# A windowed attention and an S4 convolution on one core: the planner's ranked stages replaced by one written instruction sequence per engine, with the first chunk's powers made in place, u·D kept in SBUF and QKV made by block of positions

## The chip, the cores and the metric

The kernel runs on one core of one Trainium2 chip. The metric is device time in microseconds of that core. The engines are TensorE (PE, with its weight loads shown apart as PEld), VectorE (DVE), ScalarE (ACT), GpSimd (POOL) and SyncE (SP, which here only issues DMAs).

## The reference, cut to what matters

Two independent parts, written side by side into one output of 2048 x 1280 (bf16).

```python
# A: 32 heads of 20, each position looks at 8 earlier ones, 2 apart
qkv = (x @ wqkv)                       # x 2048x640, wqkv 640x1920
idx = pos[:, None] - 2 * arange(8)
logits = einsum("bhsd,bhswd->bhsw", q, k[idx]) * 20 ** -0.5   # masked where idx < 0
a = einsum("bhsw,bhswd->bhsd", softmax(logits), v[idx]) @ wo

# B: per channel a kernel of length 2048 from 192 complex modes, then a causal convolution
P = exp(dt * A[:, :, None] * l)        # 640 channels x 192 modes x 2048
K = einsum("dn,dnl,dn->dl", C, P, dt * B).real
b = irfft(rfft(u padded) * rfft(K padded))[:2048] + u * Dskip
```

## The kernel before

Part B goes in five chunks c of 128 channels. **prep** turns the parameters into a log-magnitude `ta` and a phase `wi` (transposed by matmuls, `flip`). **am** and **gens** make the powers of exp(dt·A) for eleven exponents 2^k: ACT does an Exp and two Sin per exponent, DVE three instructions, and the result goes to the DRAM tensor `Gd`. They run twice, for chunks 0 and 1 and for chunks 2 to 4. Per chunk, **tab** and **taby** fetch the powers from `Gd` into the tables `Xg` and `Y`. **xtab** (32 DVE instructions) builds `X`, **ypos** and **yneg** (DVE) and **mag** (ACT) build the rest of `Y`. `X` has two buffers, `Xg` and `Y` have one. **kgen** multiplies X and Y in four quarters, each one zeroing matmul and 128 small ones (33 columns), and each matmul comes with its own weight load. Then POOL shuffles the result `Kd`. **u**, **spread**, **spec** (a two-step transform by matmuls, evicted by ACT), **swap** (DMA), **prod** (four DVE multiplies) and **inv** follow for each chunk. **last0** (chunks 0 to 2, spectra `Z` read back from DRAM into one buffer) and **last1** (chunks 3 and 4) make the outputs; each quarter reads its piece `uq` of u again and DVE multiplies it by Dskip.

Part A: **k0..v4** compute Q, K and V, one column block of 128 over all 2048 positions at a time, and store them in DRAM. For each of four blocks b of 512 positions, **fetch** and **fetchv** read q, k and v back (10 and 20 DMAs), **logits** has ten DVE multiplies (2048 columns) with 40 matmuls, a softmax on ACT and a DVE scaling, **av** has ten more DVE multiplies with 160 matmuls, and **out** projects by `wo`. The multiplies write one of three buffers (tag `pr`), which the matmuls then read. The pool `att` takes the memory of the prep pool, the pool `fft` that of the QKV pool, and the pool `inv` that of the tables.

Which instruction comes next on an engine is settled before the launch: a planner walks all instructions and takes ready ones by the rank of their stage in `ORDER`. Each engine then runs its list in order and waits on semaphores. Exp and Sin on ACT are pinned in program order because they use different tables.

## Time and profile before

| | |
|---|---|
| time, median of 3 runs | 466.06 us (463.52 to 466.42) |
| time recorded for the profiled execution, and its core's span | 465.34 us, 463.6 us |
| span on the page and in the trace | 468.0 us |
| mean granted TensorE clock in the trace | 0.828 of 2.4 GHz |
| busy: PE, DVE, ACT, POOL | 341.5, 309.3, 260.9, 36.7 us |

All stretches and rows are in microseconds from the start of the 468.0 us span. The profiled execution's recorded time is 2.7 us below that span, and the median of the runs is 0.7 us above the recorded time.

### The profile page before, as it was taken

To read this page: it belongs to the slowest core of one execution; us is meant where nothing else is said; L and a number is where in the kernel's file an instruction comes from. 1 tells how busy PE (TensorE), PEld (TensorE's weight loads), DVE (VectorE), ACT (ScalarE), POOL (GpSimd) and SP (SyncE) were. 2 spreads that over 40 slices of the span, in tenths; PEclk is the share of its full clock that TensorE was granted. 3 is DMA by queue.
4 is the path that set the end of the run, shared out by engine and by line. 5 is a ranking of instruction groups with operands and counts; after the bars stand their busy time and mean duration, and the time that the engine had idled before them with its cause. 6 is when DMAs were issued, how large, how long until landed. Compare 5 with 4: busy or idle time off the path is not lost.

```text
span 468.0 us, 13264 instructions
## 1 busy us (share of the span) xinstructions
PE 341.5 (73%) x5672; PEld 214.7 (46%) x5684; DVE 309.3 (66%) x448; ACT 260.9 (56%) x570; POOL 36.7 (8%) x80
## 2 busy tenths in 40 slices
...
GB/s 236 210 210 192 289 243 272 104 154 171 272 255 255 152 241 112 29 19 77 243 53 124 71 23 178 55 120 85 106 207 166 368 94 121 74 1 158 219 157 110
DMA packets 90378, 72.86 MB, mean 156 GB/s; under 512 B 44528, under 2 KB 82656, under 8 KB 88656
## 3 DMA queue, kind: packets, MB, share of 16 engines
...
## 4 chain that ended last, share of the span: by engine, by line
PE 38%; DVE 20%; DMA 16%; issue 12%; ACT 8%; SPq 4%; ACTq 0%; DVEq 0%; POOL 0%; POOLq 0%
PE ps_p L471 10%; PE ps_k L355 6%; PE ps_k L350 6%; PE ps_ia L435 4%; DVE prod L524 4%; DVE p L554 4%; DMA Gdram<-cs 4%; DMA zq<-Zdram 3%; PE ps_ib L803 3%; SPq L453 3%; DMA kd<-st 2%; DVE krtmp L265 2%; ACT mag L307 2%; ACT Sp L412 2%; DMA Xg<-Gdram 2%
## 5 line engine op out<-in xcount | busy, mean ns | idle before, releaser
L471 PE MATMUL ps_p<-xT,w 128*128 128x512 bf16 x288 | 80.2, 421 | 24.3 <-ACT st L472 15.8
L471 PEld LDWEIGHTS <-w 128*128 128x128 bf16 x300 | 30.1, 105 | 63.0 <-issue 33.9
L524 DVE TENSOR_TENSOR prod<-qb,kb 128x2048 bf16<-128x2048 bf16 x40 | 47.3, 1217 | 7.1 <-PE ps_l L528 6.0
L472 ACT CAST st<-ps_p 128x512 bf16<-128x512 f32 x60 | 34.2, 585 | 31.7 <-PE ps_p L471 23.3
L554 DVE TENSOR_TENSOR p<-vb,attn 128x2048 bf16<-128x2048 bf16 x40 | 47.1, 1217 | 2.1 <-PE ps_o L560 2.0
L408 PE MATMUL ps_f<-A,cT 64*128 64x128 bf16 (+1 forms) x768 | 36.4, 230 | 16.3 <-ACT Sp L412 8.6
L394 ACT CAST A<-ps_f 128x512 bf16<-128x512 f32 x80 | 42.1, 614 | 8.3 <-PE ps_f L393 8.1
L412 ACT CAST Sp<-ps_f 128x512 bf16<-128x512 f32 (+1 forms) x96 | 42.8, 579 | 6.0 <-PE ps_f L408 5.9
L355 PE MATMUL ps_k<-Ytab,Xtab 64*20 64x33 bf16 x1280 | 28.3, 244 | 20.2 <-issue 20.2
L408 PEld LDWEIGHTS <-cT 64*128 64x128 bf16 x768 | 31.0, 105 | 25.5 <-issue 24.7
L357 ACT CAST Kd<-ps_k 128x264 bf16<-128x264 f32 x20 | 7.5, 379 | 61.7 <-PE ps_k L355 61.7
L796 DVE TENSOR_TENSOR uq<-uq,Dsb 128x1536 bf16<-128x1536 bf16 (+1 forms) x8 | 6.6, 825 | 50.7 <-DMA uq<-Udram 37.4
L560 PE MATMUL ps_o<-p,cHs 64*32 64x256 bf16 x640 | 31.2, 308 | 11.4 <-DVE p L554 10.1
L436 ACT CAST Z<-ps_ia 128x512 bf16<-128x512 f32 x40 | 21.6, 594 | 29.6 <-PE ps_ia L435 29.5
L355 PEld LDWEIGHTS <-Xtab 64*20 64x20 bf16 x1280 | 22.3, 124 | 26.3 <-issue 24.3
L350 PE MATMUL ps_k<-Ytab,Xtab 128*20 128x33 bf16 x1280 | 28.1, 249 | 5.4 <-issue 5.4
L435 PE MATMUL ps_ia<-cE,Sp 128*128 128x128 bf16 x160 | 23.7, 244 | 9.7 <-DVE Sp L423 9.7
L350 PEld LDWEIGHTS <-Xtab 128*20 128x20 bf16 x1280 | 22.6, 128 | 12.8 <-issue 11.2
L573 PE MATMUL ps_op<-wo,oT 128*128 128x320 bf16 x160 | 27.9, 321 | 0.0
L307 ACT ACTIVATE mag<-ta 128x192 bf16<-128x192 f32 x80 | 21.7, 353 | 10.4 <-DVE Ytab L313 10.4
L264 DVE TENSOR_TENSOR Ytab<-Ytab 128x384 bf16<-128x384 bf16 (+2 forms) x15 | 13.3, 888 | 21.4 <-DMA Ytab<-Gdram 21.1
L528 PE MATMUL ps_l<-prod,cGs 128*32 128x512 bf16 x160 | 24.7, 420 | 3.2 <-DVE prod L524 3.0
...
## 6 DMA issues: line engine op xcount, KB each, us to landing
...
```

Of the source, the lines that this page charges most:

```text
L307: pin(self.nc.scalar.activation(out=self.mg[b // 8][:, b % 8], in_=ta[:, s], func=ACT.Exp, scale=-16.0 * (b + 1)))
L350: MM(o, lhsT=X[:, :, part, col], rhs=Y[:, :, part, col], start=False, stop=False, tile_position=(0, 32 * g), skip_group_check=True)
L355: MM(o, lhsT=X[hb:hb + 64, :, part - 2, col], rhs=Y[hb:hb + 64, :, part - 2, col], start=False, stop=(part == 3), tile_position=(hb, 32 * ...
L394: nc.scalar.copy(out=A1[:].rearrange("p k r s t -> p (k r) s t")[:, :, sig, 8 * q:8 * q + 8], in_=ps[:])
L408: nc.tensor.matmul(ps[h][:, kk], lhsT=C["T"][hs, k, 64 * (1 - r):64 * (1 - r) + 128], rhs=A1[hs, k, r, s0:s1, :].rearrange("p s t -> p (s ...
L412: nc.scalar.copy(out=o, in_=ps[h][:].rearrange("p k (s t) -> p s t k", t=64))
L435: nc.tensor.matmul(ps[:, i], lhsT=X[:, h, 4 * t:4 * t + 4, :].rearrange("p g k -> p (g k)"), rhs=C["E"][:, n_, :], start=(i == 0 and n_ == ...
L471: nc.tensor.matmul(ps[:], lhsT=self.w[which][:, kt, 128 * ct:128 * ct + 128], rhs=self.xT[:, kt, 512 * sc:512 * sc + 512], start=(kt == 0) ...
L472: nc.scalar.copy(out=st[:, sc], in_=ps[:])
L524: V.tensor_tensor(out=pr[:], in0=q[ct][:].unsqueeze(1).to_broadcast([128, 4, PB]), in1=windows(k[ct][:, 8 - 8 * wg:8 - 8 * wg + PB], 2, 4) ...
L554: V.tensor_tensor(out=p2[:], in0=windows(self.v[b][t][:, 2 * qp:2 * qp + 2, 0:PH], 2, 4), in1=at[:].unsqueeze(2).to_broadcast([128, 4, 2, ...
L560: nc.tensor.matmul(ps[half][32 * q:32 * q + 32, t % 2], lhsT=C["Hs"][r], rhs=p2[r, m, q2, :], start=(t % 2 == 0 and m == 0), stop=(m == 3) ...
```

## The change

`ORDER` goes. `SEQ` lists for PE, ACT, DVE, POOL and SP the stages in the order in which their instructions run, with counts: "xtab3:10" is the next ten instructions of that stage on that engine. `chain` ties each engine's instructions together in that order without semaphores.

- gens runs for chunk 0 alone and for chunks 1 to 4 together. Chunk 0's powers are written straight into `Y` and `Xg` (`here`), the others through `Gd` as before (`away`).
- Q, K and V are made by block of 512 positions (`proj(nm, sc)`), five column blocks at a time. q and k share one DRAM tensor. A block's fetch takes 5 DMAs where it took 10, its fetch of v 8 where it took 20; the two tiles of v have one buffer each.
- The loads and stores of u and the loads of HB go from SP's queue to POOL's, the loads of wqkv from POOL's to ACT's.
- u is read once into `uD` (20 KB per partition) and multiplied by Dskip in five DVE instructions of 2048 columns, in place of eight reads and eight multiplies. last0 goes in eight pieces with two halves of a buffer for the spectra.
- `flip` uses one matmul of 128 columns in place of two of 64. kgen's four quarters are stages of their own (kgen20 to kgen23 for chunk 2).

```diff
-ORDER = """
-k4 am2 inv4 v0 weights k0 u1 spec2 am0 q3 tab2 tab4 v3 prep load taby2 ypos1 ypos0 out1 xtab2 xtab0 tab1 tab0 q2 q1 swap1 k1 yneg1 load2 v2
...
+SEQ = {
+    mybir.EngineType.PE: """
...
+spec:15 out0:3 logits1:2 u1:8 logits1:2 out0:2 u1:2 out0:2 u1:2 out0 u1:2 logits1:4 u1:2 out0:2 spread0:8 out0:2 spread0:8 logits1:2 spread0:20
...
+out0:3 spec0:16 out0:2 spec0:15 out0 spec0:48 inv0:57 kgen20:129 inv0:7 logits1:8 kgen21 kgen22 kgen23:33 u2:2 logits1:2 kgen23:32 u2:2 logits1:2
+kgen23:64 u2:2 kgen22:32 u2:2 kgen22:32 u2:4 kgen22:64 u2:4 kgen21:128 spread1:36 av1:6 spread1:8 av1:5 spread1:2 av1:8 spread1:2 av1:9 spread1:2
+av1:9 spread1:2 av1:27 spec1:49 av1:15 spec1:16 av1 spec1:63 inv1:64 kgen30 kgen31:33 kgen30:32 kgen31:96 kgen30:96 kgen32 kgen33 u3:2 kgen33:32 u3:2
+kgen33:32 u3:2 kgen33:32 u3:4 kgen33:32 kgen32:32 u3:6 kgen32:32 spread2:16 kgen32:32 spread2:20 kgen32:32 av1:21 spread2:8 av1:5 spread2:2 av1:8
+spread2:4 av1:2 spread2:2 av1:12 spec2:6 logits2:4 spec2:26 av1:8 spec2 av1:19 spec2:16 av1:5 logits2:4 spec2:31 out1:2 logits2:4 spec2 out1:2
+spec2:16 out1 spec2:15 out1:2 spec2 out1:3 spec2:15 out1:20 inv2:32 out1:7 inv2:25 kgen40:33 inv2:5 logits2:4 inv2:2 out1:2 kgen40:96 logits2:4 out1
...
+out2:2 spec4:15 logits3:4 spec4 out2:2 spec4:15 logits3:4 out2:20 inv4:32 out2 logits3:4 out2:5 inv4:25 last00:18 inv4:7 logits3:12 out2:5 last01
+logits3:2 last01:8 logits3:2 last01 last02 last01:8 last02:17 last03 av3:32 last03:9 last04 last03:8 av3:17 last04:17 av3:37 last05 av3:39 last05:17
+av3:35 last06:10 out3:10 last06:8 out3:10 last07 out3:10 last07:17 last10:34 last11:17 out3:10 last11:17 last12:34 last13:34
+""",
...
+    mybir.EngineType.DVE: """
...
+xtab1:4 logits0 xtab1:4 logits0 xtab1:2 logits0 ypos1:2 logits0 ypos1:2 logits0 ypos1:2 logits0 ypos1:4 yneg1 ypos1:2 yneg1:2 u xtab2:2 yneg1 xtab2:2
+logits0 xtab2:2 logits0 xtab2:2 logits0 xtab2:2 logits0 xtab2:8 logits0 xtab2 av0:8 xtab2 av0:2 xtab2 ypos2 xtab2 logits1 xtab2:4 logits1 xtab2:4
+logits1 xtab2:2 logits1 ypos2 logits1 ypos2:2 logits1 ypos2:2 logits1 ypos2:2 logits1 ypos2 xtab3 ypos2 yneg2 ypos2:2 yneg2 xtab3 yneg2 prod0 xtab3
+prod0:2 xtab3 prod0 xtab3:2 yneg2 xtab3:2 logits1 xtab3:2 logits1 xtab3:10 logits1 xtab3:2 av1 xtab3:4 av1 xtab3:4 av1 xtab3:2 ypos3:4 av1 ypos3:2
+xtab4 ypos3:2 av1 ypos3:2 yneg3 ypos3:2 yneg3 xtab4 prod1 xtab4 prod1:2 xtab4 prod1 xtab4:2 yneg3 xtab4:2 yneg3 xtab4:2 av1 xtab4:2 av1 xtab4:2 av1
+xtab4:18 av1:2 ypos4:2 logits2 ypos4:4 logits2 ypos4:2 logits2 yneg4 ypos4 yneg4 ypos4 prod2 ypos4 prod2:2 ypos4 prod2 yneg4 logits2 yneg4 logits2:7
+av2:7 prod3:3 av2 prod3 av2 ud1 ud4 ud0 ud2 ud3 av2 logits3:6 prod4:3 logits3 prod4 logits3:4 av3:10
+""",
+    mybir.EngineType.Pool: """
+load ypos0 load:6 prep:18 load:7 ypos0 u:13 load2:4 u ypos1:2 kgen03:4 u:6 logits0:7 ypos2:2 kgen13:4 ypos3:2 kgen23:4 ypos4:2 kgen33:4 hb kgen43:4
+hb:3
+""",
+    mybir.EngineType.SP: """
+prep:12 load:15 weights k0 weights genm1:2 q0 genm1 v0 genm1:2 k1 genm1:3 q1 genm1:2 v1 genm1 k2 tab1 fetchv0:8 fetch0:2 q2 fetch0 taby1:5 v2 tab2
...
+    mybir.EngineType.SP: """
...
+inv0 swap1 u3 taby3:3 tab4 taby3:2 fetchv2:4 swap2:2 inv1 u4 taby4:5 fetchv2:4 fetch2 out1:3 fetch2 swap3:2 inv2 fetch3 out1 fetch3:2 last00:3
+last01:3 fetchv3:4 ud swap4:2 fetchv3:4 fetch3:2 out2:3 last02:3 last00:4 out2 last03:3 last04:3 last01 last02:4 last01 last05:3 last06:3 last01:2
+last03:4 last07:3 last04:4 last05:4 out3:2 last06:4 last07:2 out3 last07:2 out3 last10:4 last11:4 last12:4 last13:4
+""",
+}
+
...
-        ph = gp.tile([128, 3 * CW], i32, name="ph", tag="ph", bufs=2)[:, 0:n * CW]
-        ab = gp.tile([128, 3 * CW], f32, name="ab", tag="ab", bufs=2)[:, 0:n * CW]
-        cs = gp.tile([128, 3, 2, CW], bf16, name="cs", tag="cs", bufs=4)[:, 0:n]
+        ph = gp.tile([128, 4 * CW], i32, name="ph", tag="tmp4", bufs=4)[:, 0:n * CW]
+        ab = gp.tile([128, 4 * CW], f32, name="ab", tag="tmp4", bufs=4)[:, 0:n * CW]
+        cs, done = put(k)
         V.tensor_scalar(out=ph, in0=wi[:, s], scalar1=k + 1, scalar2=None, op0=A.logical_shift_left)
         v = lambda ap: ap.rearrange("p (c n) -> p c n", c=n)
...
-        V.tensor_tensor(out=cs, in0=cs, in1=v(am[:, k]).unsqueeze(2).to_broadcast([128, n, 2, CW]), op=A.mult)
-        (nc.sync if ca else nc.scalar).dma_start(out=Gd[ca:cb, :, G_SLOTS.index(2 ** k)].rearrange("c p r n -> p c (r n)"), in_=cs.rearrange("p c r n -> p c (r n)"))
+        with scaled():
+            V.tensor_tensor(out=cs, in0=cs, in1=v(am[:, k]).unsqueeze(2).to_broadcast([128, n, 2, CW]), op=A.mult)
+            if done:
+                done(cs)
...
+    def proj(self, which, sc):
...
+        for ct in range(5):
...
+            nc.scalar.copy(out=st[:, ct], in_=ps[:])
+        s = slice(HALO + 512 * sc, HALO + 512 * sc + 512)
+        if which == "v":
+            nc.sync.dma_start(out=self.vd[:].rearrange("h d i -> (h d) i").rearrange("(c p) i -> p c i", p=128)[:, :, s], in_=st[:])
...
+            t = p.tile([128, 2, HALO + PB], bf16, name="qk", tag="qk", bufs=3)
+            nc.sync.dma_start(out=t[:], in_=self.qkd[:, ct, :, i0:i0 + PB + HALO])
+            self.qk[b].append(t)
...
+        for i, (d0, n) in enumerate(((0, 8), (8, 12))):
+            v = p.tile([128, n, PH + 6], bf16, name="vb", tag=f"vb{i}", bufs=1)
...
+
+        for engine, text in SEQ.items():
+            left = {name: iter(made) for (e, name), made in ((k, v) for k, v in placed.items() if k) if e == engine}
+            last = None
+            for word in text.split():
+                name, _, n = word.partition(":")
+                for _ in range(int(n or 1)):
+                    ins = next(left[name])
+                    if last is not None:
+                        tc.add_manual_dep(ins, last.name, mybir.DependencyInfo(mybir.DependencyClass.NoSync, mybir.DependencyReason.DATA), reason="order of the stages")
+                    last = ins
...
+    def here(k):
+        t = tabs[0]
+        return (t.Y[:, 16 + 2 ** (k - 3)] if 3 <= k <= 7 else t.Xg[:, k if k < 3 else k - 5]).unsqueeze(1), None
+
+    def away(k):
+        cs = pp.tile([128, 4, 2, CW], bf16, name="cs", tag="cs", bufs=4)
+        return cs[:], lambda cs: nc.sync.dma_start(out=Gd[1:NCH, :, G_SLOTS.index(2 ** k)].rearrange("c p r n -> p c (r n)"), in_=cs.rearrange("p c r n -> p c (r n)"))
...
-                nc.sync.dma_start(out=us[32 * g:32 * g + 32], in_=usrc[g, :, s])
+                nc.gpsimd.dma_start(out=us[32 * g:32 * g + 32], in_=usrc[g, :, s])
...
+    with at("ud"):
+        nc.sync.dma_start(out=uD[:].rearrange("p x l t -> p (x l t)"), in_=Ud[:].rearrange("p x l t -> p (x l t)"))
+    for x in range(0, 2 * NCH, 2):
+        with at(f"ud{x // 2}"):
+            dv = Dsb[:, 16 * x:16 * x + 32].rearrange("p (x t) -> p x t", t=16).unsqueeze(2).to_broadcast([128, 2, 64, 16])
...
+    zb = fp.tile([128, 128, 32], bf16, name="zb", tag="Z")[:].rearrange("p x t -> p (x t)")[:, 0:2 * 1536].rearrange("p (b c x t) -> p b c x t", b=2, c=3, t=32)
+    for e in range(8):
+        with at(f"last0{e}"):
+            for i in range(3):
+                nc.sync.dma_start(out=zb[:, e % 2, i], in_=Zd[i][:, 16 * e:16 * e + 16])
+            inverse([0, 1, 2], zb[:, e % 2], 8 * e, 8)
```

## Rows read from the trace of the kernel before

**Rows 1.** The page's first part: busy time, share of the span and instructions of each engine.
```profile
PE 341.5 (73%) x5672; PEld 214.7 (46%) x5684; DVE 309.3 (66%) x448; ACT 260.9 (56%) x570; POOL 36.7 (8%) x80
```

**Rows 2.** Stages: engine busy us (instructions), granted clock (2.4 GHz = 1), DMA share, GB/s.
```profile
0.00:17.00 17.00, 3.46 (x34) 2.20 (x34) 1.31 (x7) 5.75 (x12) 10.57 (x25) 1.00 0.89 237
17.00:156.00 139.00, 109.27 (x1344) 53.88 (x1355) 116.41 (x212) 86.91 (x182) 15.58 (x27) 0.85 0.81 215
156.00:222.00 66.00, 43.86 (x748) 29.90 (x742) 56.12 (x79) 39.58 (x93) 3.18 (x13) 0.74 0.42 105
222.00:243.00 21.00, 13.68 (x465) 9.77 (x453) 1.44 (x5) 4.20 (x9) 2.63 (x6) 0.67 0.56 160
...
289.00:305.00 16.00, 11.18 (x342) 7.50 (x334) 0.39 (x3) 3.71 (x8) 2.62 (x6) 0.62 0.38 114
...
341.00:368.00 27.00, 17.53 (x578) 12.98 (x577) 2.75 (x3) 8.70 (x21) 2.17 (x4) 0.68 0.75 230
368.00:420.00 52.00, 45.01 (x776) 31.04 (x776) 41.63 (x37) 38.02 (x86) 0.00 (x0) 0.93 0.38 111
420.00:468.00 48.00, 29.97 (x400) 22.62 (x400) 8.43 (x10) 18.38 (x40) 0.00 (x0) 0.81 0.70 157
```

**Rows 3.** Timeline, DVE: start, length, instruction, then idle before it and its releaser.
```profile
214.16 1.22 DVE L423 TENSOR_TENSOR Sp<-Sp 128x2048 bf16<-128x2048 bf16 x1
...
242.49 0.36 DVE L264 TENSOR_TENSOR Ytab<-Ytab 128x384 bf16<-128x384 bf16 x1 [3.22 <-DMA Ytab<-Gdram]
...
278.42 1.22 DVE L423 TENSOR_TENSOR Sp<-Sp 128x2048 bf16<-128x2048 bf16 x1
...
304.69 0.36 DVE L264 TENSOR_TENSOR Ytab<-Ytab 128x384 bf16<-128x384 bf16 x1 [15.61 <-DMA Ytab<-Gdram]
...
337.27 1.21 DVE L423 TENSOR_TENSOR Sp<-Sp 128x2048 bf16<-128x2048 bf16 x1
```

**Rows 4.** Timeline, PE, first three quarters of kgen for chunk 2.
```profile
220.05 0.29 PE L343 MATMUL ps_k<-Ytab,zw 128*128 128x264 bf16 x1
...
228.29 0.65 PE L355 MATMUL ps_k<-Ytab,Xtab 64*20 64x33 bf16 x25 [3.33 <-issue]
...
234.48 0.65 PE L355 MATMUL ps_k<-Ytab,Xtab 64*20 64x33 bf16 x26 [3.23 <-issue]
```

**Rows 5.** Timeline, PE, end of kgen for chunk 4.
```profile
360.00 0.45 PE L355 MATMUL ps_k<-Ytab,Xtab 64*20 64x33 bf16 x16 [3.28 <-issue]
```

**Rows 6.** Groups by line, DVE: count | busy us, mean ns | idle before.
```profile
L524 DVE TENSOR_TENSOR prod<-qb,kb 128x2048 bf16<-128x2048 bf16 x40 | 47.3, 1217 | 7.1 <-PE ps_l L528 6.0 <-PE ps_o L560 1.1
...
L264 DVE TENSOR_TENSOR Xtab<-Xtab,Xg 128x768 bf16<-128x768 bf16 (+2 forms) x35 | 24.5, 699 | 0.5
...
L268 DVE TENSOR_TENSOR Xtab<-Xtab,krtmp 128x384 bf16<-128x384 bf16 (+2 forms) x40 | 16.2, 406 | 0.5
...
L796 DVE TENSOR_TENSOR uq<-uq,Dsb 128x1536 bf16<-128x1536 bf16 (+1 forms) x8 | 6.6, 825 | 50.7 <-DMA uq<-Udram 37.4 <-PE ps_ib L800 7.6 <-PE ps_ib L803 5.7
```

**Rows 7.** Waits of the whole span: total us, times, longest us.
```profile
ACT cs L248 <- DMA Gdram<-cs: 8.3, 5, 4.4
...
DVE cs L251 <- ACT cs L250: 5.9, 4, 3.4
```

**Rows 8.** Timeline, DVE, two single waits.
```profile
178.47 0.36 DVE L264 TENSOR_TENSOR Xtab<-Xg 128x384 bf16<-128x384 bf16 x1 [6.04 <-DMA Xg<-Gdram]
...
406.38 1.23 DVE L542 TENSOR_TENSOR attn<-attn,rc 128x1024 bf16<-128x1024 bf16 x1 [7.64 <-ACT rc L541]
```

**Rows 9.** Timeline, PE, the last 32 us.
```profile
436.83 1.52 PE L573 MATMUL ps_op<-wo,oT 128*128 128x320 bf16 x10
...
447.60 2.72 PE L803 MATMUL ps_ib<-zq,HB 128*128 128x96 bf16 x32 [5.20 <-DMA zq<-Zdram]
...
453.92 0.63 PE L803 MATMUL ps_ib<-Z,HB 128*128 128x64 bf16 x16
...
461.82 1.06 PE L803 MATMUL ps_ib<-Z,HB 128*128 128x64 bf16 x16
```

More of the change, by code (lines that the diff above doesn't have):

```diff
@@ L135, in att_consts_np @@
     return dict(Gs=gs.reshape(128, 160), Hs=hs, Sm=sm)
-ORDER = """
-k4 am2 inv4 v0 weights k0 u1 spec2 am0 q3 tab2 tab4 v3 prep load taby2 ypos1 ypos0 out1 xtab2 xtab0 tab1 tab0 q2 q1 swap1 k1 yneg1 load2 v2
-mag2 u0 yneg0 fetch0 v4 q0 spread0 k2 tab3 mag0 kgen2 mag1 gens0 kgen4 last13 q4 fetch1 spec1 inv0 kgen1 kgen0 u2 ypos2 gens2 v1 prod4 taby3
-yneg2 kgen3 k3 taby4 spec3 spec0 taby1 fetch2 ypos3 yneg4 spread3 inv3 logits0 swap0 xtab1 last10 xtab3 u3 inv2 spread1 taby0 u av3 av0
-fetchv0 swap2 last12 av2 out0 prod1 inv1 yneg3 prod2 logits3 spec xtab4 mag4 last03 u4 fetchv1 ypos4 last11 last02 last01 swap3 mag3 out3
@@ new lines @@
+v3 logits0:2 kgen11 kgen12 av0:2 u0:8 av0:2 spec:4 av0:2 spec:4 out0 spec:4 out0 spec:4 out0 u1:7 spread0:4 u1 out0 spread0:8 out0:2 spec0:6 out0
+spec0:10 mag3:14 inv0:4 mag3:2 inv0:3 out0 kgen20 inv0 logits1:2 u2:2 logits1:2 kgen23 u2:4 kgen22 u2:2 kgen21 spread1:12 av1:2 spec1:16 mag4:8 inv1:7
+mag4 inv1 mag4:7 kgen31 kgen30 u3:5 kgen33 u3:3 spread2:4 kgen32 spread2:8 av1:2 spec2:6 av1 spec2:4 av1 spec2:4 out1 spec2:2 out1:5 inv2:4 out1
+inv2:4 kgen40 out1 u4:3 kgen43 u4:4 logits2:2 u4 spread3:2 logits2 spread3 logits2 spread3 kgen42 spread3:8 kgen41 spec3:16 av2:2 inv3:4 av2:2 inv3:3
@@ L202, in weights @@
     def weights():
-        cc = pp.tile([128, 2, Wd], bf16, name="cc")
+        cc = [pp.tile([128, Wd], bf16, name="cc", tag="nat", bufs=6) for _ in range(2)]
         for i in range(2):
             for s, ps in flip(2 + i, False):
-                nc.scalar.copy(out=cc[:, i, s], in_=ps)
+                nc.scalar.copy(out=cc[i][:, s], in_=ps)
         Gt = pp.tile([128, 2, Wd], bf16, name="Gt")
```

298 lines of the change are left out of this document (154 added, 144 removed).

## The prediction

> **What bounds the kernel now.** I read the busy shares first [rows 1]: no engine is near its limit. PE is busy 341.5 of 468.0 us, DVE 309.3, ACT 260.9. So the time is made of waits, and a change of order is worth the waits that it takes away. I count them on DVE, for two reasons: every part of the work passes through it (powers, tables, products, attention), and the lengths of its instructions do not hang on the TensorE clock, so its busy time stays what it is. Its idle time is 468.0 - 309.3 = 158.7 us.
>
> The stages show where that lies [rows 2]; the reader subtracts DVE's busy time from each length. Start (0 to 17): 15.7. Powers, QKV and the first two tables (17 to 156): 22.6. To 222: 9.9. Then three stretches in which DVE does almost nothing: 222 to 243 with 19.6, 289 to 305 with 15.6, 341 to 368 with 24.2, together 59.4. 368 to 420: 10.4. The tail from 420: 39.6. That sums to 157.5; the two stretches left out hold the other 1.2.
>
> The three empty stretches are kgen of chunks 2, 3 and 4. DVE has run out of things it may do: Y has one buffer, so the next chunk's Y can be loaded only when kgen has read the old one. Its path goes from the last product (inv can start) to the loaded Y [rows 3]: 214.16 + 1.22 = 215.4 to 242.5 is 27.1 us, and 279.6 to 304.7 is 25.1 us. For chunk 4 it goes from 338.5 to the end of kgen at 360.4, 22.0 us [rows 3, 5]. A good part of it is PE waiting for nothing but its own instructions: stalls of 3.33 and 3.23 us marked "issue" [rows 4]. One leaves 25 matmuls of a quarter and the next 26, so they are 129 - 26 + 25 = 128 matmuls apart, which with their weight loads is 256 instructions. The tail is a chain of one-buffer reads: PE waits 5.20 us for the spectra [rows 9], and DVE's eight small multiplies spend 50.7 us waiting, mostly for u [rows 6].
>
> **The change part by part.** First the work itself. Counted from the code, DVE, ACT and PE keep their work: powers for 1 + 4 chunks instead of 2 + 3, the same elements in the same number of instructions. Eight multiplies with Dskip, 6.6 us, become five of 2048 columns, which by the price of such a multiply (1.217 us) are 6.1 [rows 6]. flip drops 30 small matmuls of 5684. DVE's work becomes 309.3 - 0.5 = 308.8.
>
> *The start* stays: the same parameters have to come in and be transposed before DVE has anything. 15.7.
>
> *17 to 156.* Chunk 0's powers no longer go to DRAM. ACT waited 8.3 us for such stores to free a buffer, DVE 5.9 us for ACT's second Sin [rows 7]; about half of those stores were in the first gens. Block-wise QKV lets the first 75 matmuls run on the first five transposed pieces of x. Against that, the written order puts yneg0, and so kgen of chunk 0, behind all of gens for chunks 1 to 4, and xtab1 with three logits multiplies (32 x 0.55 + 3.7 = 21 us, at the mean of 0.699 and 0.406 [rows 6]) has to cover that kgen. Bounds: 11 (both waits gone) to 29 (they stay and kgen 0 adds 6). I take 16.
>
> *156 to 222.* The wait of 6.04 us for `Xg` [rows 8] goes: in SP's list tab2 stands before block 0's last fetches, so the load starts as soon as xtab1 has read the old `Xg`. In its place the window of kgen 1, filled with 19 xtab2 instructions and 15 attention multiplies or scalings, 10 + 18 = 28 us, about as long as the path of the other kgens. Bounds 4 to 14; I take 8.
>
> *The three kgen windows*, the heart of it. I count what the list gives DVE between the last product and the first instruction that needs the finished kgen. Chunk 2: 28 xtab3 instructions, a sign flip, three logits and three av multiplies: 15.4 + 0.6 + 7.3 = 23.3 against a path of 27.1, so 4 idle. Chunk 3: 28 xtab4, two of yneg3, five av: 15.4 + 2.3 + 6.1 = 23.8 against 25.1, 1 idle. Chunk 4: two of yneg4, eight of logits2, then three av2 (the fourth has no `pr` buffer until PE, which has almost all of kgen in front, has read the first): 2.3 + 9.7 + 3.7 = 15.7 against 22.0, 6 idle. But the written PE order also puts 16 u matmuls and 12 to 20 attention matmuls inside each kgen, and they can only partly hide in the stalls: I add 3, 5 and 5. Together 24 in place of 59.4. Bounds: 5 (the added matmuls all hide in the stalls) to 45 (the path grows by 7 us per window).
>
> The Trainium skill (Runtime: NRT & Kernel Launch, section Instruction fetch mechanics) says that instructions come in blocks of 256 and that crossing a border is mostly hidden. The trace has the block [rows 4] and contradicts "hidden" where small matmuls follow each other; what the page would make of the time is the second rival.
>
> *368 to 420* has what depends on softmax: 7.64 us before the last scaling [rows 8]. The list still ends logits3 with a scaling that needs PE, then Ln and Exp on ACT, and only then av3; nothing else is left for DVE. 10.4 becomes 12, bounds 8 to 18.
>
> *The tail.* Six of last0's eight pieces now stand beside logits3 and av3, u·D is there from one read, and two halves of a buffer take the spectra. After DVE's last multiply PE has 16 av matmuls, two pieces of last0, 40 of out3 and last1: 0.6 + 2.9 + 6.1 + 8.5, at 1.52 per ten for out, 2.72 per 32 for last0 and 0.63 to 1.06 per 16 for last1 [rows 9]. From the last matmul's end at 462.9 to 468.0 there are 5.1 us of copy, store and end. That is 23 in place of 39.6. Bounds 18 to 30.
>
> *Costed at nothing:* SP has fewer DMAs to issue (by count 317 become 236). POOL issues 24 more and 3 fewer; at its mean of 0.46 us (36.7 / 80 [rows 1]) that is 11 us on an engine idle for 431. What is queued there: kgen 0's shuffle stands behind the second u store, which waits for a DVE copy placed at yneg0's end, and logits0's masks behind the last u store; both are needed later than that. If the cover fails, spread0 starts late by one wait, some 5 us. The DMA engines are 0.81 busy from 17 to 156 [rows 2] and I take nothing from the change of queue there.
>
> *Sum.* 15.7 + 16 + 8 + 24 + 1.2 + 12 + 23 = 99.9 idle, plus 308.8 busy, is a span of 408.7. The profiled execution's recorded time is 2.7 below its span: 406.
>
> **The rivals.** *The windows stay half open.* The multiplies moved beside kgen wait for a buffer that PE frees only behind kgen, and spec and spread queue behind the same kgen. For it: the three-buffer limit and PE's busy 13.7 of 21 in such a stretch [rows 2]. Against it: xtab needs no PE. Windows at 45, tail at 28: 406 + 21 + 5 = 432.
>
> *The instruction stalls hide.* Attention matmuls mixed into kgen give the fetch time to run ahead. For it: outside kgen PE is 0.87 busy from 368 to 420 with 776 matmuls [rows 2] and needs no such waits. Against it: 128-matmul runs of pure kgen remain. Windows at 5 and 3 less before: 406 - 22 = 384. By the Runtime page's "mostly hidden" this is the case to expect; the stalls of 3.3 us [rows 4] speak against it.
>
> *Slower, through PE's clock.* The finer mixing makes PE wait in order for DVE and ACT at many more places, and the granted clock falls towards 1.2 GHz. The same 16 matmuls take 0.63 us in one place and 1.06 in another [rows 9], and the clock was 0.62 to 0.68 in the stretches with waits and 0.93 in the dense one [rows 2]. PE's 341.5 us at a mean of 0.83 become 472 at 0.60; with 17 us before and 5 after them, 494, so about 490. It decides from a mean of 0.64: 443 + 22 = 465. Against it: the order removes long PE waits rather than adding them.
>
> *It does not do what it says:* before and after are both fixed lists, and if DMA sets the pace (0.81 busy to 156, 0.75 and 0.70 in two of the late stretches [rows 2]), the waits only change their names: about 462.
>
> **How the numbers follow.** Forecast (395 to 420) 0.52, half-open windows 0.22, hidden stalls 0.15, slower 0.06, no effect 0.05. The unknowns do not all fall to one side: the range goes from 380, under the hidden stalls, to 440, over the half-open windows. Runs differ by 0.6%, so 1% is about what this kernel's times can tell from no change. Faster by over 1% (below 461): the first three, 0.89; within 1%: 0.04; slower: 0.07.
>
> **What would show it.** Right: no DVE gap over 9 us beside kgen of chunks 2 to 4; DVE's last multiply some 23 us before the end; busy time within 2 us of 308.8; xtab3 and av1 running while kgen 2 does. Wrong: gaps of 15 us still there with "PE ps_k" or "DMA Ytab" behind them; a mean granted clock under 0.7; new waits of DVE on `pr` buffers summing to more than 20 us; PE waiting for chunk 0's table later than 105 us.

## The result, and the profile after

The changed kernel took 418.26 us (median of 4; 417.12 to 422.12) beside 464.88 us for the kernel before on the same chip: a ratio of 0.901 (95% interval 0.894 to 0.908). Run again with the experiments it took 418.84 us (7 runs, 412.64 to 424.16), ratio 0.889 (0.884 to 0.895). Ratios leave out executions more than 1.5% above the fastest of their kernel; medians hold all. The forecast was 406, so the direction, the range and most of the mechanism held, and the gain is 12 us smaller than predicted.

The page's first part, then the stages (length, busy time of each engine, granted clock, DMA share, GB/s; they answer to [rows 1, 2]):

```profile
span 415.1 us, 13105 instructions
...
PE 316.8 (76%) x5645; PEld 196.1 (47%) x5654; DVE 307.1 (74%) x445; ACT 262.1 (63%) x570; POOL 50.4 (12%) x101
```

```profile
0.00:17.00 17.00, 4.17 (x30) 2.32 (x30) 2.52 (x9) 4.92 (x14) 9.81 (x21) 1.00 0.78 135
17.00:156.00 139.00, 102.92 (x1160) 49.49 (x1170) 114.88 (x207) 86.42 (x177) 27.86 (x48) 0.89 0.84 204
156.00:222.00 66.00, 56.37 (x1149) 36.66 (x1151) 59.19 (x80) 47.33 (x113) 3.06 (x13) 0.84 0.60 160
222.00:300.00 78.00, 63.90 (x1512) 45.59 (x1501) 67.93 (x99) 55.31 (x120) 5.26 (x12) 0.85 0.42 115
300.00:390.00 90.00, 75.14 (x1569) 51.23 (x1569) 62.55 (x55) 56.52 (x124) 4.45 (x8) 0.94 0.66 194
390.00:415.10 25.10, 14.33 (x244) 10.82 (x243) 0.00 (x0) 11.64 (x27) 0.00 (x0) 0.86 0.61 120
```

DVE's busy time moved by 2 us, as it should in a change of order; its idle time fell from 158.7 to 108.0. Subtracting busy from length, stage by stage: 14.5, 24.1, 6.8, 10.1, 27.4, 25.1. The stretch from 222 to 300 holds the waits beside the kgens of chunks 2 and 3 (PE works on them from 214.9 to 232.9 and from 258.9 to 278.6). These two kgens cost DVE 19.6 and 15.6 us of idle time before; now DVE is 0.87 busy in the whole stretch. PE's granted clock rose from a mean of 0.83 to 0.89 (2.4 GHz is 1), and its busy time fell by 25 us.

DVE's longer gaps, from its timeline (the gap stands in brackets, with what ended it; answers to [rows 3, 8]):

```profile
102.34 0.36 DVE L306 TENSOR_TENSOR Xtab<-Xg 128x384 bf16<-128x384 bf16 x1 [4.53 <-DMA Xg<-Gdram]
...
119.51 1.24 DVE L562 TENSOR_TENSOR prod<-qk 128x2048 bf16<-128x2048 bf16 x1 [2.57 <-DMA qk<-qkd]
...
131.85 1.23 DVE L562 TENSOR_TENSOR prod<-qk 128x2048 bf16<-128x2048 bf16 x1 [6.03 <-PE ps_l L566]
```

```profile
222.77 1.22 DVE L580 TENSOR_TENSOR attn<-attn,rc 128x1024 bf16<-128x1024 bf16 x1
...
225.65 1.22 DVE L592 TENSOR_TENSOR p<-vb,attn 128x2048 bf16<-128x2048 bf16 x1
...
237.06 0.36 DVE L306 TENSOR_TENSOR Ytab<-Ytab 128x384 bf16<-128x384 bf16 x1 [4.01 <-DMA Ytab<-Gdram]
...
279.04 1.23 DVE L592 TENSOR_TENSOR p<-vb,attn 128x2048 bf16<-128x2048 bf16 x1 [4.35 <-PE ps_o L598]
...
319.95 1.23 DVE L580 TENSOR_TENSOR attn<-attn,rc 128x1024 bf16<-128x1024 bf16 x1 [6.85 <-ACT rc L579]
...
334.13 1.23 DVE L466 TENSOR_TENSOR UT<-Sp,UT 128x2048 bf16<-128x2048 bf16 x1 [4.32 <-ACT Sp L456]
...
347.06 5.77 DVE L886 TENSOR_TENSOR uD<-uD,Dsb 128x2048 bf16<-128x2048 bf16 x5 [5.90 <-DMA uD<-Udram]
...
376.75 1.22 DVE L580 TENSOR_TENSOR attn<-attn,rc 128x1024 bf16<-128x1024 bf16 x1 [3.45 <-ACT rc L579]
```

While kgen 2 runs (214.9 to 232.9) DVE scales block 1's attention and makes its first value products; the next Y still arrives at 237, but only 4.0 us of that path are uncovered, in place of 19.6. The gap beside kgen 3 is 4.4, and beside kgen 4 (301.8 to 326.1) there are two, of 2.8 and of 6.9, the latter a wait for the softmax. New is the wait of 5.90 at 347.06: the resident u·D, a step that I had costed at nothing.

PE in the kgen of chunk 0, which stands in the list almost as one block (nine matmuls of q stand behind its first quarter), and in that of chunk 2, into which u's matmuls are mixed (answers to [rows 4]):

```profile
104.87 0.44 PE L398 MATMUL ps_k<-Ytab,Xtab 128*20 128x33 bf16 x13 [1.08 <-issue]
...
113.54 0.44 PE L398 MATMUL ps_k<-Ytab,Xtab 128*20 128x33 bf16 x13 [6.03 <-issue]
...
120.56 0.44 PE L398 MATMUL ps_k<-Ytab,Xtab 128*20 128x33 bf16 x13 [4.38 <-issue]
```

```profile
223.82 0.44 PE L437 MATMUL ps_f<-cBU,U 128*128 128x256 bf16 x2
224.19 0.73 PE L398 MATMUL ps_k<-Ytab,Xtab 128*20 128x33 bf16 x32
...
229.22 0.44 PE L437 MATMUL ps_f<-cBU,U 128*128 128x256 bf16 x2 [2.15 <-issue]
...
232.67 0.24 PE L403 MATMUL ps_k<-Ytab,Xtab 64*20 64x33 bf16 x2 [0.61 <-issue]
```

Chunk 0's stalls marked "issue", 1.08, 6.03 and 4.38 us, stand 128 matmuls apart, the longer two well above the 3.33 and 3.23 of [rows 4]. Chunk 2's are 2.15 and 0.61, 2.8 in all. And what the DMA engines did beside chunk 0's kgen, where "instruction" is a kind of traffic of its own on the same engines, though of 0.8% (and 0.3% on a second such queue):

```profile
q1 hardware_dynamic: 5680, 4.74, 57.4%
q0 software_dynamic: 1102, 3.20, 36.4%
q8 instruction: 4, 0.07, 0.8%
```

### The profile page after: what moved, and what is told of

The parts are those of the page before. It is cut to its first block, busy times and chain, and to the rows that moved or that the text cites. A ratio compares the mean times of both kernels' runs of the same rounds, so it can differ in the third digit from the quotient of the medians.

```text
span 415.1 us, 13105 instructions
## 1 busy us (share of the span) xinstructions
PE 316.8 (76%) x5645; PEld 196.1 (47%) x5654; DVE 307.1 (74%) x445; ACT 262.1 (63%) x570; POOL 50.4 (12%) x101
## 5 line engine op out<-in xcount | busy, mean ns | idle before, releaser
L515 PE MATMUL ps_p<-xT,w 128*128 128x512 bf16 x291 | 76.4, 409 | 20.9 <-ACT st L516 15.4
L562 DVE TENSOR_TENSOR prod<-qk 128x2048 bf16<-128x2048 bf16 x40 | 48.2, 1225 | 11.6 <-PE ps_l L566 8.9
L592 DVE TENSOR_TENSOR p<-vb,attn 128x2048 bf16<-128x2048 bf16 x40 | 47.4, 1224 | 12.1 <-PE ps_o L598 12.0
L516 ACT CAST st<-ps_p 128x512 bf16<-128x512 f32 x60 | 34.6, 586 | 23.1 <-PE ps_p L515 21.1
L398 PE MATMUL ps_k<-Ytab,Xtab 128*20 128x33 bf16 x1280 | 29.7, 248 | 15.1 <-issue 15.1
L598 PE MATMUL ps_o<-p,cHs 64*32 64x256 bf16 x640 | 27.7, 297 | 12.5 <-DVE p L592 7.7
L452 PE MATMUL ps_f<-A,cT 64*128 64x128 bf16 (+1 forms) x768 | 29.4, 211 | 5.4 <-ACT Sp L456 3.5
L479 PE MATMUL ps_ia<-cE,Sp 128*128 128x128 bf16 x160 | 25.5, 254 | 8.0 <-DVE Sp L467 7.8
L452 PEld LDWEIGHTS <-cT 64*128 64x128 bf16 x768 | 21.7, 96 | 18.4 <-issue 17.1
L403 PE MATMUL ps_k<-Ytab,Xtab 64*20 64x33 bf16 x1280 | 27.4, 244 | 3.5 <-issue 3.5
L479 PE MATMUL ps_ia<-cE,UT 128*128 128x128 bf16 x160 | 25.4, 253 | 0.0
L306 DVE TENSOR_TENSOR Xtab<-Xtab,Xg 128x768 bf16<-128x768 bf16 (+2 forms) x35 | 24.5, 699 | 0.3
L307 DVE TENSOR_TENSOR krtmp<-Xtab,Xg 128x768 bf16<-128x768 bf16 (+2 forms) x35 | 24.4, 698 | 0.0
```

What stands on the lines that cost most here:

```text
L398: MM(o, lhsT=X[:, :, part, col], rhs=Y[:, :, part, col], start=False, stop=False, tile_position=(0, 32 * g), skip_group_check=True)
L403: MM(o, lhsT=X[hb:hb + 64, :, part - 2, col], rhs=Y[hb:hb + 64, :, part - 2, col], start=False, stop=(part == 3), tile_position=(hb, 32 * ...
L452: nc.tensor.matmul(ps[h][:, kk], lhsT=C["T"][hs, k, 64 * (1 - r):64 * (1 - r) + 128], rhs=A1[hs, k, r, s0:s1, :].rearrange("p s t -> p (s ...
L479: nc.tensor.matmul(ps[:, i], lhsT=X[:, h, 4 * t:4 * t + 4, :].rearrange("p g k -> p (g k)"), rhs=C["E"][:, n_, :], start=(i == 0 and n_ == ...
L515: nc.tensor.matmul(ps[:], lhsT=self.w[which][:, kt, 128 * ct:128 * ct + 128], rhs=self.xT[:, kt, 512 * sc:512 * sc + 512], start=(kt == 0) ...
L516: nc.scalar.copy(out=st[:, ct], in_=ps[:])
```

## The experiments

**The changed kernel again**, to have a base for what is run beside it.

> The changed kernel once more, unaltered, as the base for the kernels that are run beside it. Its median was 418.3 us (417.1 to 422.1). Theory: 417 to 419, and the same stretches of DVE idle time in the trace (14 us from 96 to 132, 25 us after the last multiply). Rival: the stalls of PE in kgen of chunk 0 (1.08, 6.03 and 4.38 us) were chance of one execution; then they are of other sizes here.

Median 418.84. Chunk 0's stalls were 1.08, 6.29 and 4.11: they belong to the kernel, not to one execution. DVE's idle time from 96 to 132 was 14.0 again. What differed was the wait for u·D: 11.89 us in place of 5.90, in an execution whose span was 422.2 instead of 415.1. Of the 7.1 us between these two executions 6.0 are this one wait.

**u's read ahead of block 3's value loads.**

```
-last01:3 fetchv3:4 ud swap4:2 fetchv3:4 ...
+last01:3 ud fetchv3:4 swap4:2 fetchv3:4 ...
```

> In SP's list the read of u for the resident u D goes ahead of the first four value loads of block 3, behind which it stood; nothing else. In the changed kernel's trace SP sat at those value loads from 316.4 to 326.4 (their buffer was in use), the read was issued at 329.4 and DVE waited 5.90 us for it at 341.2. Theory: the read is issued some 10 us earlier, the wait goes, and since the PE work behind DVE's next attention multiply is dense up to 376 the end moves by 4 to 6 us: 412 to 414. Rival one: the load only shares the DMA engines with the 4 MB of HB and lands no earlier, no change, 418. Rival two: the value loads of block 3 or the softmax chain (3.45 us at 376) take the time back: 416 to 418.

407.13 us (6 runs), ratio 0.874 (0.870 to 0.878), clear of the changed kernel's 0.884 to 0.895: 11.7 us less by the medians, 7.3 by the ratios, more than the 4 to 6 that I expected either way. Between the two traces it is 10.1 us (spans of 405.0 and 415.1), but 3.8 of them were there before the edit could act, since the wait for `Xg` ended at 98.54 here and at 102.34 in the changed kernel. SP and POOL in the changed kernel, then here (DMA issues: start, time from the first issue to the end of the last, count):

```profile
326.44 2.90 SPq L551 DMA_DIRECT2D vb<-vd  x4
329.44 0.43 SPq L882 DMA_DIRECT2D uD<-Udram  x1
```

```profile
326.39 0.60 POOL L879 DMA_DIRECT2D HB<-k_HB  x1 [44.82 <-PE ps_k L403]
```

```profile
321.68 0.32 SPq L882 DMA_DIRECT2D uD<-Udram  x1
322.09 2.93 SPq L551 DMA_DIRECT2D vb<-vd  x4
```

```profile
321.91 0.60 POOL L879 DMA_DIRECT2D HB<-k_HB  x1 [45.13 <-PE ps_k L403]
```

The theory's effect is there, its reason is not: the read is not issued 10 us earlier. In both kernels SP's next issues, and HB's, begin within 0.4 us of the end of chunk 4's kgen (326.07, here 321.59), whose memory u and HB take over. In the changed kernel u stands 3.05 us behind HB's first of four loads of 1 MB each and lands 17.5 us after its issue (23.1 in the repeated run); here it is 0.23 us ahead of HB, lands after 10.4, and DVE has no wait for it. The four value loads pay for it: they land 21.5 us after their issue in place of 7.5, and nothing in the trace waits for them. So the gain is that the load which is needed first goes first. Rival one ("lands no earlier") falls. The edit puts u ahead of the value loads and of HB at once; which of the two held it back is not shown.

**v's matmuls mixed into chunk 0's kgen.** ACT's copies follow.

```
-kgen03:129 kgen02:128 kgen01:128 v2:25 ...
+kgen03:33 v2:3 kgen03:32 v2:3 kgen03:32 v2:3 kgen03:32 v2:3 kgen02:32 v2:3 kgen02:32 ...
```

> PE's list only (and the order of ACT's copies that follow from it): the 25 matmuls of v for block 2, which stood behind kgen of chunk 0, are put between its groups of 32 small matmuls, two or three at a time. In the changed kernel's trace that kgen, unmixed, had stalls marked issue of 1.08, 6.03 and 4.38 us, 128 matmuls apart; kgens 2 to 4, with other matmuls in between, had 0 to 3.4 us together. Theory: mixing with long matmuls is what takes the stalls away; they fall from 11.5 to under 4 us, kgen with v takes some 22 us instead of 24.5 and 8.3 behind it, DVE's waits at 117 to 132 shrink by 5 to 8 us, and the end comes 4 to 7 us earlier: 411 to 414. Rival: the stalls come from the DMA engines, which are 0.95 busy from 96 to 132 against 0.31 to 0.66 at the later kgens; then they stay at 9 to 14 us and the time at 418, or above it, since the table is ready later.

416.53 us, ratio 0.885 (0.879 to 0.891): not told from the changed kernel by its time. The stalls fell to 0.45, 3.04, 0.36 and 1.18, 5.0 together, between theory and rival. The wait for `ps_l` of 6.03 at 131.85 was gone, but the softmax wait was 11.12 and the wait for u·D 12.62, at 348.89, where the changed kernel has the same instruction at 347.06. The gain ran into u's late read.

**Two of four output stores on POOL's queue.**

```
-            nc.sync.dma_start(out=dst_b[g, :, s, ...
+            (nc.sync, nc.gpsimd)[g % 2].dma_start(out=dst_b[g, :, s, ...
```

> Of the four output stores of each piece of the inverse, two are issued by POOL instead of all four by SP; nothing else. In the changed kernel's trace PE's last matmul starts at 405.54, but SP issues 16 stores one behind the other from 403.31 for 9.2 us (0.575 each). Theory: the end hangs on SP's list, so the last eight issues leave it and the end comes 4 to 5 us earlier: 413.5 to 414.5. Rival: the stores themselves (2.0 us each, DMA share 0.61 there) or ACT's last copies set the end: 418, no change. A third: POOL's issues are dearer (0.9 us for each of the two to three seen at 95.84 and 96.70) and the end is 1 to 2 us later.

421.12 us, ratio 0.895 (0.890 to 0.901): no gain. From the last softmax wait's end to the end it is 39.8 us (380.92 to 420.7) beside 38.3 (376.75 to 415.1). SP's last stores in the changed kernel and here, then ACT and POOL here:

```profile
403.31 9.20 SPq L902 DMA_DIRECT2D out_dram<-ysb  x16
```

```profile
406.45 8.06 SPq L902 DMA_DIRECT2D out_dram<-ysb  x8
...
407.82 1.07 ACT L900 CAST ysb<-ps_ib 128x512 bf16<-128x512 f32 x2 [1.40 <-DMA out_dram<-ysb]
...
409.18 1.29 POOL L902 DMA_DIRECT2D out_dram<-ysb  x2 [1.18 <-ACT ysb L900]
```

The rows of SP run from the first issue to the last and hold the waits between them. A single issue takes SP 0.32 to 0.57 us in the changed kernel and 0.32 to 0.50 here, so it did not become dearer; the 1.01 that I took from 8.06 / 8 counts the waits. What the stores wait for here is the ring of two buffers: a piece starts every 2.3 to 2.5 us (406.45, 408.92, 411.25, 413.66), SP and POOL wait for ACT's copy, and two of the last three copies wait for a store to free their buffer. And with the last stores on POOL the span ends 5.5 us after the last issue (415.2 and 420.7), with all of them on SP 2.6 us after it (412.5 and 415.1).

**The parts without the written lists.** The lists go, and the stages get the old ranks (for instance `kgen20` to `kgen23` that of kgen2, u·D that of the first piece of the inverse).

```
-    chain()
+ALIAS.update({f"kgen{c}{q}": f"kgen{c}" for c in range(5) for q in range(4)})
+        name = ALIAS.get(name, name)
+        save, tc.cur_priority = tc.cur_priority, 1000 * RANK[name]
```

> The changed kernel's parts (first-chunk powers in place, blockwise QKV, wider fetches, resident u D, half pieces of the inverse, the changed queues) without its written lists: the stages are ordered by the planner and the ranking of the kernel before, each new stage at its old stage's rank. Theory (the prediction's): the parts are worth a few us at the start and some 10 in the tail, the order the rest, so 440 to 455, with DVE gaps of 15 us and more still beside kgen of chunks 2 to 4. Rival: the parts carry the gain and the list only fixes an order that the planner would find too: 418 to 430. A second rival: parts without their order are worse than before (resident u D read late, HB from the slower queue): 465 to 480.

517.46 us, ratio 1.109 (1.103 to 1.115): slower than before by 51 us, on the side of the second rival and far past its figure.

```profile
17.00:100.00 83.00, 54.82 (x226) 22.84 (x230) 49.21 (x97) 54.66 (x104) 21.03 (x33) 0.85 0.93 197
...
468.00:514.70 46.70, 19.79 (x244) 15.21 (x241) 0.00 (x0) 9.45 (x21) 0.00 (x0) 0.64 0.51 107
```

```profile
283.96 3.52 DVE L514 TENSOR_TENSOR prod<-qk 128x2048 bf16<-128x2048 bf16 x3 [15.50 <-PE ps_l L518]
...
412.27 2.36 DVE L544 TENSOR_TENSOR p<-vb,attn 128x2048 bf16<-128x2048 bf16 x2 [16.78 <-PE ps_o L550]
```

DVE's busy time is the same 308.7; it idles 206.1 in place of 158.7. Gaps of 15.5 and 16.8 us stand in the middle, 33.8 of the 83 us from 17 to 100 are idle (12.1 in the old trace), and the last 46.7 us have nothing for DVE at all. So the parts alone are worth less than nothing under this ranking, and the list is worth 99 us to them. A ranking made for the new parts might do better; that wasn't tried.

**The windows emptied again.** On the kernel with u's read ahead:

```
-... xtab3:2 logits1 xtab3:2 logits1 xtab3:10 logits1 ...
+... xtab3:2 logits1 xtab3:2 logits1 gate2 xtab3:10 logits1 ...
-... xtab4:2 yneg3 xtab4:2 yneg3 xtab4:2 av1 ...
+... xtab4:2 yneg3 xtab4:2 yneg3 gate3 xtab4:2 av1 ...
+V.tensor_copy(out=gs[0:20].rearrange("p (b t) -> p b t", t=8), in_=Kds[c + 2][0:20, c, 0:4, ...])
```

> On the kernel with u's read moved ahead (407.1 us). DVE gets one small copy beside kgen of chunk 2 and one beside kgen of chunk 3, which read the finished table; behind them stand, in the list's order, what had filled these two windows (22 xtab instructions, a scaling and three av multiplies; 24 xtab instructions and five av multiplies). No other work is added. Theory: the two windows open again, DVE's gaps there go from 3.7 each to some 15 to 20 each, and the time rises by most of that, 20 to 32 us: 427 to 439. Rival: by now PE or the softmax chain sets the pace in these stretches and DVE had slack; the rise is under 10: 407 to 417.

436.43 us (434.99 to 441.46; ratio 0.938) beside 407.13 (0.874): 29.3 us, as the theory has it. The two gaps:

```profile
227.28 0.16 DVE L862 COPY gs<-Kd 20x32 bf16<-20x32 bf16 x1 [17.20 <-ACT Kd L406]
...
285.03 0.16 DVE L862 COPY gs<-Kd 20x32 bf16<-20x32 bf16 x1 [20.77 <-ACT Kd L406]
```

17.2 and 20.8, in place of 3.7 and 3.7: 30.6 us of idle time, and nearly all of it reaches the end. What fills these two windows is worth half of the 58 us between the kernel with u's read ahead and the kernel before.

**Chunk 2's kgen as one block.** On the same kernel:

```
-inv0:7 logits1:8 kgen21 kgen22 kgen23:33 u2:2 logits1:2 kgen23:32 u2:2 ... kgen22:64 u2:4 kgen21:128 spread1:36
+inv0:7 logits1:12 kgen21 kgen22 kgen23:129 kgen22:128 kgen21:128 u2:16 spread1:36
```

> On the kernel with u's read moved ahead. PE's list puts the three last quarters of kgen of chunk 2 into one block of 384 small matmuls; the 16 u and 4 logits matmuls that stood between them stand before and behind it. Read for its trace: in the changed kernel this kgen, mixed, has no stall marked issue over 1 us. Theory: mixing hides the stalls; unmixed, with the DMA engines no busier than before, stalls of 1.5 to 3.5 us come back every 128 matmuls, 5 to 8 us in all, and kgen 2 ends that much later. Rival: it was the quiet DMA engines (some 0.6 in that stretch, against 0.95 at kgen of chunk 0) that took them away; then none comes back and the path stays within 1 us.

One execution, 411.36 us.

```profile
222.04 1.10 PE L397 MATMUL ps_k<-Ytab,Xtab 128*20 128x33 bf16 x50 [4.40 <-issue]
...
225.76 1.10 PE L397 MATMUL ps_k<-Ytab,Xtab 128*20 128x33 bf16 x50 [1.06 <-issue]
```

```profile
236.12 0.36 DVE L305 TENSOR_TENSOR Ytab<-Ytab 128x384 bf16<-128x384 bf16 x1 [9.03 <-DMA Ytab<-Gdram]
```

The stalls are back: 4.40 and 1.06, against 1.84 and 0.68 with u mixed in. (That the mixed kgen has none over 1 us, as I wrote beforehand, was misread: the changed kernel has one of 2.15.) The block ends at 228.1, the mixed kgen at 227.2 from the same start, though that one holds u's 16 matmuls too (3.2 us by themselves here); a wait of 0.7 us ahead of four logits matmuls came with the block's order. With u's matmuls behind it the same work is done at 231.2, 3.9 us later. The next table is ready 9.03 us late for DVE, not 3.7, and that is the order's doing more than the stalls': SP's list has the next read of u ahead of the table, it is issued at 231.19, as u's matmuls end, and the table at 231.61 in place of 227.31.

**Useless traffic beside chunk 2's kgen.** On the same kernel, three times:

```
+                    nc.gpsimd.dma_start(out=Wd[i][:], in_=tabs[2].Y[:, 0:8])
```

> On the kernel with u's read moved ahead. POOL's queue issues three copies of eight slots of chunk 2's Y to spare DRAM (786 KB each) when that Y is complete, that is when its kgen begins; they serve nothing. Read for its trace. Theory: with other matmuls mixed in, kgen hides its stalls even beside busy DMA engines: under 2 us of them, and kgen 2 as long as before. Rival: instruction blocks come through the same DMA engines, so the stalls of chunk 0's kgen (6.03, 4.38) come from the traffic there, and 3 us and more of stall shows here too. In both cases the next Y may land later, since it shares the engines.

One execution, 408.26 us. The stalls are 1.56, 1.54 and 0.16, 3.3 in all beside 2.5, and kgen ends 2.2 us later from the same start (within 0.2), with 5.3 MB instead of 3.1 moved in some 20 us. "As long as before" did not hold: 0.7 of the 2.2 us are stall, and PE's busy time grew from 15.4 to 16.8 us, at a granted clock of 0.83 in place of 0.87. Mixed matmuls cover most of the stalls: the rival's "3 us and more" is just reached in the sum, in none of the stalls.

**Less traffic beside chunk 0's kgen**, still one block. On the same kernel:

```
-tab1 fetchv0:8 fetch0:2 q2 fetch0 taby1:5 v2 tab2 ...
+tab1 fetch0:2 q2 fetch0 taby1:5 fetchv0:8 v2 tab2 ...
-... u:13 load2:4 u ypos1:2 kgen03:4 u:6 ...
+... u:14 ypos1:2 kgen03:4 load2:4 u:6 ...
```

and two of DVE's u copies stand later in its list.

> On the kernel with u's read moved ahead. PE's list stays; kgen of chunk 0 is still one block. What DMAs run beside it is less: the fetches of v for block 0 (1.3 MB) go behind chunk 1's Y in SP's list, the output weights (0.8 MB) behind chunk 0's shuffle in POOL's, and DVE's second and third u copies (and the 1.3 MB that follow each) some 15 us later. Read for its trace. Theory: mixing, not traffic, is the main thing, since chunk 2's kgen as one block had 4.40 and 1.06 us of stall with engines no busier than before; but the surplus of chunk 0's (6.0 to 6.3 and 3.6 to 4.4 and 1.1 to 1.4, 11 to 11.5 together) is traffic, so 6 to 9 us of stall, and DVE's wait for q and k at 117 (2.6) shorter. Rival one: traffic is nothing, 11 us as before. Rival two: traffic is all, under 4 us.

```profile
102.14 0.44 PE L397 MATMUL ps_k<-Ytab,Xtab 128*20 128x33 bf16 x13 [1.51 <-issue]
...
106.69 0.45 PE L397 MATMUL ps_k<-Ytab,Xtab 128*20 128x33 bf16 x13 [1.91 <-issue]
...
110.42 0.44 PE L397 MATMUL ps_k<-Ytab,Xtab 128*20 128x33 bf16 x13 [1.09 <-issue]
```

The stretch from 95 to 125 here, then in the kernel without the edit:

```profile
95.00:125.00 30.00, 25.49 (x580) 14.65 (x570) 23.04 (x43) 8.81 (x19) 9.06 (x15) 0.83 0.70 162
```

```profile
95.00:125.00 30.00, 18.43 (x518) 12.21 (x509) 20.00 (x38) 6.63 (x15) 8.40 (x15) 0.72 0.96 225
```

4.5 us of stall in place of 11.2, with a DMA share of 0.70 in place of 0.96 in that stretch, and of 0.49 beside the kgen itself (94.5 to 112.1): more than the theory gave to traffic, close to rival two. The block of chunk 2 had 5.5 us at a share of 0.47. Both things count, then: traffic made chunk 0's stalls long, and a block of small matmuls is what lets any show. The trace's DMA packets show what the stalls wait for: each ends 1.3 to 1.7 us after a packet of 16 KB of the kind "instruction" has landed. In the changed kernel's chunk 0 these land at 103.36, 111.87 and 119.24 (the stalls end at 104.87, 113.54 and 120.56), in chunk 2's block at 220.42 and 224.34 (222.04 and 225.76), here at 100.65, 105.33 and 109.11 (102.14, 106.69 and 110.42). From one landing to the start of the next such packet it is 6.1 and 7.1 us beside the full engines, 2.6 to 3.7 in this run and in chunk 2's block; the packet itself takes 0.9 to 1.5. So the stalls are the fetch of instructions, and the packets start later beside traffic; when they are asked for, the trace does not show.

The one execution took 415.16, 8 us more than without the edit: what was moved away came back as waits for chunk 2's powers (3.90, at 143.56), for logits (5.55, at 155.79) and for u (2.02).

**Both useful edits, and the tail's buffers.** The first kernel has u's read ahead and v mixed into kgen 0; the second gives the last four pieces three output buffers; the third adds POOL's stores to that.

```
-        ysb = ip.tile([128, 1024], bf16, name="ysb", tag="ysb", bufs=2)[:, ...
+        ysb = (ip.tile([128, 1024], ..., bufs=2) if n == 3 else a.p.tile([128, 2048], bf16, name="ysb", tag="pr", bufs=3))[:, ...
```

> The read of u ahead of block 3's value loads and v's matmuls mixed into kgen of chunk 0, both together, nothing else. Alone they gave 407.1 and 416.5 beside 418.8. Theory: in the run with the mixing alone DVE was 9 us ahead up to 303 and lost it again in longer waits for the softmax (11.1 in place of 7.1) and for u (12.6); with u there in time most of the 9 comes through: 398 to 402. Rival: the softmax wait keeps what it took and only 2 to 3 come through: 404 to 405.

> The two mended kernel, and the last four pieces of the inverse get three output buffers of their own (in the attention products' place, which is free by then) instead of two shared ones; SP still issues all stores. In the trace ACT's last copies wait up to 2.2 us for a store to free a buffer. Theory: SP's 16 stores, 9.2 us one behind the other, are the limit, so ACT runs ahead and nothing changes at the end: within 1 us of the two mended kernel. Rival: the copy waits for a store, the store for the copy, and it is this ring of two that sets the pace: 2 to 4 us less.

> The kernel with these three buffers, and two of each piece's four output stores issued by POOL. With two buffers the split gave nothing (tail from DVE's last softmax wait to the end 39.8 us beside 38.3): SP's issues went from 0.575 to 1.01 us each, and ACT waited for buffers 1.3 to 1.4 us per piece. Theory one: both limits had to go together, SP's list and the ring of two; then the end comes 2 to 4 us earlier than in the two mended kernel. Theory two: the rate at which stores of 128-byte and 192-byte runs are written out is the limit, whoever issues them: four stores per piece still take some 2.3 us, and the time is within 1 us of the two mended kernel, or above.

404.40, 404.03 and 403.00 us; ratios 0.869 (0.863 to 0.876), 0.872 (0.864 to 0.880), 0.866 (0.858 to 0.874). All three beat both kernels; they aren't told from each other, nor for certain from the kernel with u's read alone. My 398 to 402 for the first rested on a wrong reading: part of those "9 us ahead" was there before the edit could act, since the wait for `Xg` ended at 96.04 in that execution and at 100.88 in the base. Against the kernel with u's read alone, where that wait ends at the same time (98.54 and 98.53), mixing puts DVE 4.0 us ahead at 303 (303.26 and 307.23) and 2.2 at the end.

In the tail buffers changed nothing, as expected. With three buffers and both queues the stores were issued earlier, SP's list in the first two rows, POOL's last pair in the third:

```profile
391.07 9.18 SPq L902 DMA_DIRECT2D out_dram<-ysb  x16
```

```profile
389.93 6.74 SPq L902 DMA_DIRECT2D out_dram<-ysb  x8
```

```profile
395.95 1.29 POOL L902 DMA_DIRECT2D out_dram<-ysb  x2 [1.91 <-ACT ysb L900]
```

The last issue ends at 397.2 instead of 400.3, and by the DMA engines' slices the last store traffic near 399.1 instead of 401.4, but the span ends 5.6 us after the last issue instead of 2.6. That is what the run with two queues showed (5.5), so what splitting the stores gains is lost there. What lies in these last microseconds no view shows; that stays open.

## Why the prediction was right, and where it was off

The terms of the sum, each with what it measured (us, in the profiled execution):

| term | forecast | measured |
|---|---|---|
| DVE busy | 308.8 | 307.1 |
| start, 0 to 17 | 15.7 | 14.5 |
| 17 to 156 | 16 | 24.1 |
| 156 to 222 | 8 | 6.8 |
| windows of chunks 2 and 3, and rest | 14.2 | 10.1 |
| window of chunk 4, and softmax | 11 + 12 | 27.4 |
| tail | 23 | 25.1 |
| span | 408.7 | 415.1 |
| recorded time less span | -2.7 | +2.0 |
| time | 406 | 417.1 |

**The heart of it held.** The windows of chunks 2 and 3 closed to 4.0 and 4.4 us, beside 4 and 1 by the count of what the list gives DVE to do, and opening them again costs 29.3 us. The list carries the gain: the same parts without it are slower than before. The rival "windows half open" needs gaps of 15 us that aren't there. DVE's waits on attention products are these, before (with the two in the first line of [rows 6]) and after (total us, times, longest):

```profile
DVE p L554 <- PE ps_o L560: 2.0, 3, 1.3
```

```profile
DVE p L592 <- PE ps_o L598: 12.0, 8, 4.4
...
DVE prod L562 <- PE ps_l L566: 8.9, 2, 6.0
```

That is 20.9 us after, but 9.1 before, with the 6.0 and 1.1 of [rows 6]. So 11.8 are new, well under the 20 that I had set as a border, and one of 6.03 is chunk 0's kgen and not a window.

**The windows' addition wasn't there, as far as it was tested.** "I add 3, 5 and 5" for the matmuls mixed into kgen: in chunk 2 they cost nothing. As one block the same kgen has twice the stall and ends no earlier. Chunk 3's gap of 4.4 lies between the count (1) and the sum (6), and the attention products end it, not the table; no run separates it. The rival that the stalls hide was thus half right, and for its own reason, "attention matmuls mixed into kgen give the fetch time to run ahead". Its price didn't follow, since the gain was lost elsewhere. The Trainium skill (Runtime: NRT & Kernel Launch, section Instruction fetch mechanics) calls the crossing of a block mostly hidden: the runs come near it for mixed matmuls (2.5 us left in chunk 2's whole kgen, 5.0 in chunk 0's beside busy DMA engines) and contradict it for blocks of small ones (5.5, and 11.5 beside busy DMA engines).

**The term for 17 to 156 failed by 8 us.** It took chunk 0's kgen to be covered by 21 us of DVE work. The kgen with its 9 other matmuls took 24.5 (97.7 to 122.2), 11.5 of it stall, because the list puts it as one block where the DMA engines are 0.95 busy; v's matmuls stand behind it and logits behind those, hence the wait of 6.03. Less traffic took the stalls to 4.5, mixing to 5.0. The waits for `Xg` (4.5) and for q and k (2.6), in the same stretch, were not in the sum either. I looked at the DMA share (0.81) and took nothing from it; here it was part of the term.

**"u·D is there from one read", costed at nothing, cost 5.9 to 13.1 us in the four traces that have it late.** I followed the read out of the tail but not to its new place: behind block 3's value loads on SP, and beside 4 MB of HB, on engines that serve both. Moved ahead of them, the time is 407.1, one microsecond from the forecast, though with other terms that are off still in it. In the table above it is more than the excess of 4.4 in the row of chunk 4's window.

**The tail** was 2 us over. PE was done sooner than I had added up, 16.4 us after DVE's last multiply in place of 18.1, but from the end of its last matmul (406.2) to the end (415.1) it is 8.9 us: SP's 16 stores run from 403.3 to 412.5. I had read 5.1 us of "copy, store and end" off the old trace as a constant. Neither a second queue nor more buffers shortened it.

**The last step, "minus 2.7",** had the wrong sign: the recorded time lies 1.7 to 2.1 us above the core's span in every execution listed, of both kernels. I had set the page's span of 468.0 against a recorded 465.34, beside which the list has a span of 463.6; the page was of another execution.

**The slower rival** didn't come: the clock's mean went up, to 0.89, far from its 0.64.
